# An adaLN block on one core: attention units, their background work, and where three of its jobs are put

## The chip, the cores and the metric

The kernel runs on one core of one Trainium2 chip. The metric is the device time of one execution in microseconds. The core has five engines with queues of their own: TensorE (PE, with PEld for its weight loads), VectorE (DVE), ScalarE (ACT), GpSimd (POOL), and SyncE (SP), which here issues nearly all DMAs.

## The reference

One transformer block with adaptive layer norms: S = 2048 tokens, D = 512, 32 heads of 16, F = 1792, all in fp32.

```python
mod = (_silu(c) @ w_mod).reshape(c.shape[0], 6, 1, -1)
sa, ca, ga, sb, cb, gb = (mod[:, 0], mod[:, 1], mod[:, 2], mod[:, 3], mod[:, 4], mod[:, 5])
h = _layernorm(x, axis=-1) * (1 + ca) + sa
x = x + ga * _A_ref(h, A_wqkv, A_wo)          # qkv, softmax(q k^T / 4) v, times wo
h = _layernorm(x, axis=-1) * (1 + cb) + sb
x = x + gb * _B_ref(h, B_w1, B_b1, B_w2, B_b2)  # gelu(h w1 + b1) w2 + b2
```

## The kernel before

Each large product is made of three products of the high and low parts of its factors (`terms3`): high·high, high·low, low·high.

**Units and half steps.** The attention is cut into 32 units: a block of 512 queries times a group of 4 heads (`NG` = 8 groups to a block, `NB` = 4 blocks). A unit has 16 half steps, so the main loop runs 512 (`half_step`). A half step issues on PE: 4 score matmuls `e`, transposed, keys by queries, with the exponential on ScalarE behind each; 4 score matmuls `mx` of a later unit (80 ahead, `LEAD`), with a reduction to the row's maximum on VectorE behind each; up to 6 background matmuls `bg`, on the two halves of the array's rows; and at its end the 4 matmuls `pv` of the half step before (`pv_step`), which the trace shows as 8 records. The maxima of a unit go through `max_rows` to DRAM (`m`) and from there into two rows of `qst`, so that the score matmul subtracts them itself. After the last `pv` of a unit `attn_out` copies the bank `pv` to `osb`, and a DMA takes it to `ou` in DRAM.

In the last 20 half steps there are no `mx` left; the code calls this "ending".

**Background.** A generator, `work`, hands out jobs: first the projections of q, k and v that are still missing (`block0`), then for each block of tokens the output projection with its layer norm (`front`) and the feed-forward (`feed`). A job is a group of matmuls into one bank; a group of 24 half-row matmuls takes four half steps. Where a generator yields nothing, because what it needs isn't there, the half step has no background. What is left when the loop is over runs in the tail on the full array, and there the last block follows: its output projection (`part_o`, bank `o`), layer norm and feed-forward. The numbers of `feed` groups in the tail are those that the loop didn't get to.

**Clock.** `advance` counts 4 per half step. `later(n, f)` runs f n counts on; `soon(n, f)` likewise, in its own order. All engines are fed in the order in which the program is written, so such a delay is a place in an engine's queue, and an instruction that must wait holds up what stands behind it there.

**Heads before the output projection.** When two groups of a block are out, a pair goes to `ready`, 8 counts after its `osb`; `o_prep(b, k)` then loads the sums `dn` and the values `ob` from `ou`, takes the reciprocal on VectorE (`inv`, 14 counts later, 20 for the first three of block 0), stores it to `rden` (`store`), loads it spread over rows (`load`, `rb`) and divides on GpSimd (`div`, 7 counts after the load). `done[b]` counts what is divided; `front` waits until all four are, and 4 counts more.

**Weights.** `wload` issues the next load of the list `stream` into one of 8 slots (`WB`), as soon as a slot has been dropped. Before the change the four tiles of wo for block b+1 stand ahead of the last part of block b's feed-forward weights. `open_ffn` opens the pool in which these slots lie, once the projections' own pools can be closed; the first four tiles of wo follow it.

**Layer norm of `front`.** Behind each of four groups the evacuation (`y`), the addition to x, the statistics in two halves on VectorE (`stat`, moved by `calm` where `max_rows` has just been), and the normalisation `xn`; then four transposes (`trans`), for block 0 as jobs of their own in empty half steps, for the others as `sides`, in a bank of the ring `mx` beside a half step's work.

Of the kernel before, what the change touches and what calls it, by code (L numbers as in the profile page):

```python
# [10 lines left out]
AF = mybir.ActivationFunctionType  # L11
# [11 lines left out]
NF = FF // P  # L23
# [36 lines left out]
Y202.a X1 x*2  # L60
"""
RUN = 6
WB = 8
FIRST = {"h32": 4, "pf": 1, "vr": 3}
STAGE = {"pf": 1, "vr": 1, "wraw": 2, "wf": 1}
# [6 lines left out]
def block_kernel(ctx: ExitStack, tc: tile.TileContext, x, wqkv, wo, w1, b1, w2, b2, c, w_mod, out):  # L72
# [233 lines left out]
        hi, lo = ([a[:, i].rearrange("p (k q c) -> p q k c", q=4, k=4) if blocks else a[:, i] for i in n] for a in hT[b])  # L306
        return terms3([t[:, 0, i] for i in n], [t[:, 1, i] for i in n], hi, lo)

    def proj_qk(w, k, b):
        def evac(ps):  # L310
            parts, r = pieces("parts"), stage("pf")
            ac.activation(r, ps, AF.Copy)
            gp.tensor_copy(parts[:, 0], r)
            gp.tensor_tensor(parts[:, 1], r, parts[:, 0].bitcast(F32), op=ALU.subtract)
            soon(6, lambda: store_qk(w, k, b, parts))

        return proj_terms(w, k, b), "bg", evac

# [378 lines left out]
        return act  # L697

    done = [-1] * NB
    ready = []  # L700

    def attn_out(u, pv):
        qb, g = divmod(u, NG)
        o = kqpool.tile([P, TB], F32, tag="osb", name="osb", bufs=1)
        saw(ac.activation(o, pv, AF.Copy))  # L705
        late = u < NU - 1
        later(2 * late, lambda: sy.dma_start(ou_d[qb][g], o))
        if g % 2:
            later(8 * late, lambda: ready.append((qb, g // 2)))

    def pv_step():
        s = cur["pv"]
# [38 lines left out]
    def o_prep(b, k):  # L751

        dn = small.tile([P, 32], F32, tag="dn", name="dn")
        base = ou_d[b]
        sy.dma_start(dn, base[2 * k : 2 * k + 2].rearrange("g (j r) (a f) -> (g j) r a f", r=32, f=32)[:, DH])
        ob, rb = tmp("ob"), tmp("rb")
        for g in range(2):
            sy.dma_start(ob[g * 64 : (g + 1) * 64], base[2 * k + g].rearrange("(j r) t -> j r t", r=32)[:, :DH])
        eng = ve if over[0] else gp
        r = rden_d[b][k * 8 : (k + 1) * 8]  # L760
        busy[0] += 1

        def inv():
            ve.reciprocal(dn, dn)
            later(0 if over[0] else 2, store)

        def store():
            sy.dma_start(r.rearrange("h (a f) -> (h a) f", f=32), dn)
            later(1 if over[0] else 5, load)
            if over[0]:  # L770
                wload()

        def load():
            sy.dma_start(rb, bass.AP(tensor=r.tensor, offset=r.offset, ap=[[TB, 8], [0, DH], [1, TB]]))
            later(9 if over[0] else 7, div)
            if over[0]:
                for _ in range(6):
                    wload()
                load_x2(last, x2)

        def div():
            eng.tensor_tensor(ob, ob, rb, op=ALU.mult)
            eng.tensor_copy(pc(b, k, 0), ob)
            eng.tensor_tensor(pc(b, k, 1), ob, pc(b, k, 0).bitcast(F32), op=ALU.subtract)
            done[b] += 1
            busy[0] -= 1

        later(11 if over[0] else 20 if b == 0 and k < KC - 1 else 14, inv)

    def try_prep():  # L790
        if not ready or not pcs:
# [15 lines left out]
    for b in range(NB):  # L807
        at = 0
        for lo, hi, top in PARTS:
            if hi == NF and b < NB - 2:  # L810
                stream += [(b + 1, "o", k) for k in range(KC)]
            stream += [(b, 1, i) for i in range(at, top)] + [(b, 2, i) for i in range(lo, hi)]
            at = top
        if b == NB - 2:
            stream += [(b + 1, "o", k) for k in range(KC)]
    wt, used, ringed, extra = {}, set(), [], []

# [34 lines left out]
    def front(b, x2):  # L852


        later(9, lambda: load_x2(b, x2))
        yield from until(lambda: done[b] == KC - 1)
        yield from wait(4)
        yield from loaded(b, *[("o", k) for k in range(KC)])
        mv = small.tile([P, 4, 2], F32, tag="mv", name="mv")
        rs = {}  # L860
        xn = {}

        def norm(t):
            xn[t] = tmp("xn")
            (gp if b or t < 3 else ve).tensor_scalar(
                xn[t], x2[t], mv[:, t, 0:1], rs[t], op0=ALU.subtract, op1=ALU.mult)
            later(40, lambda: gp.tensor_tensor(x2[t], x2[t], b2_b, op=ALU.add))
            if b and len(xn) == 4:
                later(9, lambda: sides.extend([lambda fc=fc: trans(fc, "mx") for fc in range(KC)]))

        def stat(t):
            if b == 0 and t == 3:
                ln_stat(mv, t, x2[t])
                later(1, lambda: factor(t))
                return
# [12 lines left out]
            calm(lambda: [part(0), later(4, lambda: calm(lambda: [part(1), later(4, whole)]))])  # L888

        def factor(t):  # L890
            rs[t] = small.tile([P, 1], F32, tag=f"rt{t}", name=f"rt{t}")
            ve.tensor_scalar(rs[t], mv[:, t, 1:2], EPS, None, op0=ALU.add)
            gp.tensor_tensor(rs[t], rs[t], mhalf[:, 0:1], op=ALU.pow)
            later(3 if t < 3 else 2, lambda: norm(t))

        for t in range(4):

            def evac(ps, t=t):
                y = tmp("y")
                ac.activation(y, ps, AF.Copy)  # L900

                def add():
                    gp.tensor_tensor(x2[t], y, x2[t], op=ALU.add)
                    later(8 if b or t < 3 else 3, lambda: stat(t))
# [5 lines left out]
        t0 = clock["t"]  # L910

        def trans(fc, bk="bg"):
            ps = take(bk)
            for t in range(4):
                te.transpose(ps[:, t * P : (t + 1) * P], xn[t][:, fc * P : (fc + 1) * P], ident)  # L915
            h = tmp("h32")
            ac.activation(h, ps, AF.Identity, scale=modc[:, 1, fc, 0:1], bias=modc[:, 1, fc, 1:2])
            gp.tensor_copy(pc(b, fc, 0), h)
            gp.tensor_tensor(pc(b, fc, 1), h, pc(b, fc, 0).bitcast(F32), op=ALU.subtract)
            turned[fc] = clock["t"]  # L920

        turned = {}
        yield "ln"
        if b:
            yield from until(lambda: len(turned) == KC and clock["t"] >= turned[KC - 1] + 8)
            return
        yield from until(lambda: len(xn) == 4 and clock["t"] >= t0 + 9)
        for fc in range(KC):
            yield lambda fc=fc: trans(fc)
        yield from wait(4)  # L930

    def feed(b, x2):

# [47 lines left out]
        for lo, hi, top in PARTS:  # L981
# [11 lines left out]
            for t in range(4):  # L993
                sl = slice(t * P, (t + 1) * P)

                def evac(ps, t=t):
                    add_x2(ps, t)
                    if hi == NF:
                        r0 = b * TB + t * P
                        later(2 if over[0] else 8, lambda: sy.dma_start(out[r0 : r0 + P, :], x2[t]))  # L1000

                yield [(gt[i][0][:, a, sl], wt[b, 2, i][:, c]) for i in range(lo, hi) for a, c in three], "bg", evac
            drop(b, *[(2, i) for i in range(lo, hi)])

    def block0():
# [13 lines left out]
        for n, (w, k, bs) in enumerate(plan):  # L1019
            if not pcs and not any(0 in p[2] for p in plan[n:]):  # L1020
                open_pc()
            yield from until(lambda: (w, k) in wt_of)
            fetch(n + 2)
            for b in bs:
                yield proj_v(k, b) if w == 2 else proj_qk(w, k, b)
            wt_of.pop((w, k))
        yield from until(lambda: not preps and not owed[0] and not blocked and not vrows and not busy[0])
        open_ffn()

    pools["old"] = [dvcm, scm, wcm, hcm]  # L1030

# [2 lines left out]
    def work():  # L1034
# [3 lines left out]
        for b in range(NB - 1):  # L1038
            for j in fronts[b]:
                if j != "ln":  # L1040
                    yield j
            for j in feed(b, pools["x2"][b % 2]):
                if j != "last":
                    togo[0] -= b == NB - 2 and j is not None
                    yield j
                elif b < NB - 2:
                    for i in fronts[b + 1]:
                        if i == "ln":
                            break
                        yield i  # L1050

    jobs = work()
    act = {"g": None}
# [290 lines left out]
```

## Time and profile before

| | |
|---|---|
| runs | 1674.72, 1675.60, 1676.36 us; median 1675.6 |
| profiled execution | 1677.1 us |
| its span | 1675.3 us |
| granted TensorE clock, mean | 0.997 |
| busy: PE, PEld | 1654.6 us (99%), 899.8 us (54%) |
| busy: DVE, ACT, POOL | 1406.9 us (84%), 1227.6 us (73%), 701.6 us (42%) |
| DMA | 246.95 MB, 147 GB/s on average |
| VectorE's reductions L419 | 2034 of 681 ns |
| ScalarE's exponentials L691 | 2048 of 609 ns |
| ScalarE's copies `osb` L705 | 32 of 601 ns |

Times in rows are microseconds from the start of the span. A row of the timeline gives start, duration, engine, line, operation, output and inputs, shape and count, and in brackets how long the engine stood before it and what released it. PE's matmuls are pipelined, so neighbouring rows overlap, and the start of one `pv` burst to the start of the next is the length of a half step.

### The profile page before, as it was taken

The numbers are of one execution on the slowest core, as the hardware profiler recorded it, in microseconds if no ns is written. First come the engines' busy times: TensorE is split into PE (matmuls) and PEld (weight loads), VectorE is DVE, ScalarE is ACT, GpSimd is POOL, SyncE is SP. The second block draws the span as 40 slices with busy tenths as digits, with TensorE's granted clock in tenths as the row PEclk, the third lists the DMA queues.
The fourth block names the chain that finished last, engine by engine and source line by source line (L and its number), as shares of the span: only waits on it lengthen the run. The fifth ranks groups of instructions, "written<-read, shape, count | busy, mean of one in ns | idle before, by whom it ended". The sixth has DMA issues, their size and how long they took to land.

```text
span 1675.3 us, 32208 instructions
## 1 busy us (share of the span) xinstructions
PE 1654.6 (99%) x12055; PEld 899.8 (54%) x12055; DVE 1406.9 (84%) x2734; ACT 1227.6 (73%) x2352; POOL 701.6 (42%) x705
## 2 busy tenths in 40 slices
PE   7999999999999999999999999999999999999999
PEld 6655555555554455555545555555545555553777
DVE  7899899998898998898999888998999888890432
ACT  4357777777777788778877888778877788779131
POOL 8343544535121556306533456306533366226110
PEclk9999999999999999999999999999999999999999
DMA  9766766766447444336363364345363453233544
GB/s 298 204 198 181 229 206 208 226 178 199 140 138 213 119 106 116 77 83 167 96 168 87 101 162 119 81 106 157 101 170 88 123 143 99 70 117 97 218 151 154
DMA packets 142808, 246.95 MB, mean 147 GB/s; under 512 B 25391, under 2 KB 53053, under 8 KB 142653
## 3 DMA queue, kind: packets, MB, share of 16 engines
q1 hardware_dynamic: 140896, 243.80, 50.4%
q8 instruction: 95, 1.56, 0.4%
q10 hardware_dynamic: 1756, 1.11, 0.3%
q14 instruction: 61, 0.49, 0.1%
HBM read 184.56 MB, written 60.29 MB: 146 GB/s over the span
## 4 chain that ended last, share of the span: by engine, by line
PE 94%; DVE 2%; DMA 2%; ACT 2%; issue 0%; SPq 0%; POOL 0%; POOLq 0%; DVEq 0%; ACTq 0%
PE bg L278 40%; PE pv L717 29%; PE e L684 17%; PE mx L414 4%; PE pr L278 2%; ACT p L691 1%; DVE mxp L419 1%; PE o L278 1%; PE warm L466 1%; DMA w2s<-wsp 1%; DMA dn<-ou 0%; DVE bst L236 0%; PE mx L915 0%; DMA qk<-parts 0%; DMA wo<-wos 0%
## 5 line engine op out<-in xcount | busy, mean ns | idle before, releaser
L419 DVE TENSOR_REDUCE mxp<-mx 128x1 f32<-128x512 f32 x2034 | 1284.8, 681 | 128.2 <-PE mx L414 108.5
L691 ACT ACTIVATE p<-e 128x512 f32<-128x512 f32 x2048 | 1073.1, 609 | 275.6 <-PE mx L414 233.1
L414 PE MATMUL mx<-kh,qst 48*128 48x512 f32 x2034 | 836.6, 423 | 0.7 <-DVE mxp L419 0.5
L684 PE MATMUL e<-qst,kh 50*128 50x512 f32 x2048 | 779.5, 424 | 3.3 <-ACT p L691 3.3
L684 PEld LDWEIGHTS e<-qst,kh 50*128 50x128 f32 x2048 | 341.8, 185 | 438.3 <-ACT p L691 325.6
L717 PE MATMUL pv<-p,vg 128*17 128x512 f32 x4096 | 540.0, 598 | 0.3 <-ACT osb L705 0.3
L414 PEld LDWEIGHTS mx<-kh,qst 48*128 48x128 f32 x2034 | 368.2, 185 | 16.2 <-DVE mxp L419 9.3
L278 PE MATMUL bg<-w,g 64*128 64x512 f32 (+1 forms) x1056 | 264.4, 389 | 0.0
L278 PEld LDWEIGHTS bg<-w,g 64*128 64x128 f32 (+1 forms) x1056 | 196.0, 186 | 29.0
L278 PE MATMUL bg<-pchi,w 64*128 64x512 f32 (+1 forms) x656 | 178.0, 391 | 0.0
L717 PEld LDWEIGHTS pv<-p,vg 128*17 128x17 f32 x4096 | 68.2, 95 | 174.3 <-issue 171.8
L278 PE MATMUL bg<-hThi,wqkv 64*128 64x512 f32 x560 | 153.4, 393 | 0.2 <-DVE tick L1149 0.2
L278 PEld LDWEIGHTS bg<-pchi,w 64*128 64x128 f32 (+1 forms) x656 | 120.9, 185 | 23.4 <-DVE tick L1127 4.3
L278 PEld LDWEIGHTS bg<-hThi,wqkv 64*128 64x128 f32 x560 | 103.7, 186 | 12.7 <-DVE tick L1149 0.5
L959 POOL TENSOR_SCALAR s<-s 128x512 f32<-128x512 f32 x40 | 59.9, 1497 | 101.8 <-ACT s L957 101.4
L978 POOL TENSOR_TENSOR x<-y,x 128x512 f32<-128x512 f32 x28 | 36.0, 1286 | 148.0 <-ACT y L977 148.0
L278 PE MATMUL bg<-pclo,w 64*128 64x512 f32 (+1 forms) x328 | 88.9, 389 | 0.0
L278 PE MATMUL bg<-hTlo,wqkv 64*128 64x512 f32 x280 | 76.2, 391 | 0.0
L952 POOL TENSOR_TENSOR s<-h 128x512 f32<-128x512 f32 x40 | 41.7, 1042 | 65.2 <-ACT h L951 65.2
L278 PEld LDWEIGHTS bg<-pclo,w 64*128 64x128 f32 (+1 forms) x328 | 60.0, 184 | 13.2 <-DVE tick L1127 4.3
L278 PE MATMUL bg<-wo,pchi 64*128 64x512 f32 x192 | 60.2, 394 | 1.6 <-DMA wo<-wos 1.6
L278 PEld LDWEIGHTS bg<-hTlo,wqkv 64*128 64x128 f32 x280 | 51.6, 184 | 7.7
(165 smaller groups left out, 1313.6 us busy)
## 6 DMA issues: line engine op xcount, KB each, us to landing
kh<-qk SPq DMA_DIRECT2D x256, 192.0 KB
w<-w1s SPq DMA_DIRECT2D x56, 512.0 KB
w<-w2s SPq DMA_DIRECT2D x54, 512.0 KB
qk<-parts SPq DMA_DIRECT2D x32, 512.0 KB
vg<-v SPq DMA_DIRECT2D x48, 272.0 KB
qst<-qk SPq DMA_DIRECT2D x64, 192.0 KB
qk<-parts SPq DMA_DIRECT2D x32, 256.0 KB
ou<-osb SPq DMA_DIRECT2D x32, 256.0 KB
```

The source lines that it names most:

```text
L278: return te.matmul(ps, term[0][r], rhs, start=i == 0, stop=i == n - 1)
L414: te.matmul(ps, qst[u][r0 : r0 + KR, p, qc * P : (qc + 1) * P], kh(u, kr // 2)[r0 : r0 + KR, p, (kr % 2) * TB : (kr % 2 + 1) * TB], start= ...
L419: ins = ve.tensor_reduce(mxp[u][:, hc, kr : kr + 1], ps, axis=AX.X, op=ALU.max, negate=True)
L466: te.matmul(warm[:, :P], ident, ident, start=True, stop=True)
L684: ins = te.matmul(ps, kh(u, kc // 8)[r0 : r0 + KX, p, (kc % 8) * P : (kc % 8 + 1) * P], qst[u][r0 : r0 + KX, p], start=True, stop=True)
L691: op = ac.activation(t, ps, AF.Exp, scale=SCALE)
L717: te.matmul(pvb[32 * j : 32 * j + VW], vg[u % 2][:, n : n + VW], pt.pop(4 * s + j), start=kc == 0, stop=kc == NKC - 1)
L952: gp.tensor_tensor(s, h, h, op=ALU.mult)
L959: gp.tensor_scalar(s, s, 1.0, None, op0=ALU.add)
L978: later(4, lambda: gp.tensor_tensor(x2[t], y, x2[t], op=ALU.add))
```

## The change

Six things change, and no computation is left out.

- `attn_out` copies the bank `pv` to `osb` on VectorE rather than ScalarE, and `calm` takes note of it.
- The chain of the heads: for the last pair of blocks 1 and 2, ready 4 counts rather than 8 after `osb`, reciprocal 9 rather than 14, division 3 rather than 7; for the first three pairs of block 0, reciprocal 28 rather than 20. `front` no longer waits for the division plus 4 counts, but for a mark set 2 counts after the load of `rb`.
- wo's tiles: for block 0 the four loads are issued right behind `open_ffn`, that is when the pools change, followed by a wait of 12 counts (`OPEN`); the last projection's store goes out at once, so that the pool can open. For the later blocks wo(b+1) stands behind all of block b's weights in the list, and is asked for at the yield "last".
- `work` lets the feed-forward of block b go on with a group wherever the front of block b+1 has nothing yet at its beginning.
- The transposes of block 0, too, go into `sides`, 5 rather than 9 counts after the last `xn`, and `front` goes on when three of four have been issued.
- Delays of statistics and of the addition of b2 are changed, and the slots of w2 of a block's last part are dropped one after another.

```diff
+OPEN = 12
-    def proj_qk(w, k, b):
+    def proj_qk(w, k, b, last=False):
-            soon(6, lambda: store_qk(w, k, b, parts))
+            soon(0 if last else 6, lambda: store_qk(w, k, b, parts))
...
+    close_by = [False] * NB
...
-        saw(ac.activation(o, pv, AF.Copy))
+        saw(ve.tensor_copy(o, pv))
+        rowed[0] = clock["t"]
         late = u < NU - 1
         later(2 * late, lambda: sy.dma_start(ou_d[qb][g], o))
         if g % 2:
-            later(8 * late, lambda: ready.append((qb, g // 2)))
+            later((4 if 0 < qb < NB - 1 and g == NG - 1 else 8) * late, lambda: ready.append((qb, g // 2)))
...
-            later(9 if over[0] else 7, div)
+            later(9 if over[0] else 3 if fast else 7, div)
+            if k == KC - 1:
+                later(2, lambda: close_by.__setitem__(b, True))
...
-        later(11 if over[0] else 20 if b == 0 and k < KC - 1 else 14, inv)
+        fast = 0 < b < NB - 1 and k == KC - 1
+        later(11 if over[0] else 28 if b == 0 and k < KC - 1 else 9 if fast else 14, inv)
...
-            if hi == NF and b < NB - 2:
-                stream += [(b + 1, "o", k) for k in range(KC)]
             stream += [(b, 1, i) for i in range(at, top)] + [(b, 2, i) for i in range(lo, hi)]
             at = top
-        if b == NB - 2:
+        if b < NB - 1:
             stream += [(b + 1, "o", k) for k in range(KC)]
...
-        yield from until(lambda: done[b] == KC - 1)
-        yield from wait(4)
+        yield from until(lambda: close_by[b])
...
-            later(40, lambda: gp.tensor_tensor(x2[t], x2[t], b2_b, op=ALU.add))
-            if b and len(xn) == 4:
-                later(9, lambda: sides.extend([lambda fc=fc: trans(fc, "mx") for fc in range(KC)]))
+            later(40 if b else 72, lambda: gp.tensor_tensor(x2[t], x2[t], b2_b, op=ALU.add))
+            if len(xn) == 4:
+                later(5, lambda: sides.extend([lambda fc=fc: trans(fc, "mx") for fc in range(KC)]))
...
-            calm(lambda: [part(0), later(4, lambda: calm(lambda: [part(1), later(4, whole)]))])
+            n = 4 if t < 3 else 3
+            calm(lambda: [part(0), later(n, lambda: calm(lambda: [part(1), later(n, lambda: calm(whole))]))])
...
-        if b:
-            yield from until(lambda: len(turned) == KC and clock["t"] >= turned[KC - 1] + 8)
-            return
-        yield from until(lambda: len(xn) == 4 and clock["t"] >= t0 + 9)
-        for fc in range(KC):
-            yield lambda fc=fc: trans(fc)
-        yield from wait(4)
+        yield from until(lambda: len(turned) >= KC - 1)
...
+                if t == 3 and hi == NF and b < NB - 2:
+                    for n, i in enumerate(range(lo, hi)):
+                        later(7 + 4 * n, lambda i=i: drop(b, (2, i)))
...
         open_ffn()
+        for k in range(KC):
+            wload()
+        yield from wait(OPEN)
...
-            for j in feed(b, pools["x2"][b % 2]):
+            fd = feed(b, pools["x2"][b % 2])
+            for j in fd:
...
                 elif b < NB - 2:
+                    first = True
+                    for k in range(KC):
+                        wload()
                     for i in fronts[b + 1]:
                         if i == "ln":
                             break
-                        yield i
+                        first = first and i is None
+                        yield next(fd) if first else i
```

How this moves instructions, at three places. On SP, ahead of unit 9, where block 0's wo is asked for. `qk<-parts` are the projection's last stores, `m` and `qst<-m` the maxima on their way, `kh` keys, `w` tiles of w1. Before:

```order
L301 DMA qk_86<-parts 128x512
L441 DMA m_104<-m_7429 4x32x32 x2
L300 DMA qk_86<-parts 128x2x512
L301 DMA qk_86<-parts 128x512
L447 DMA qst<-m_104 2x1024 x2
L386 DMA kh_194<-qk_88 48x2x512 x2
L831 DMA wo<-wos_135 128x1024
```

Now:

```order
L301 DMA qk_86<-parts 128x2x512
L302 DMA qk_86<-parts 128x512
L835 DMA wo<-wos_135 128x1024
L835 DMA wo<-wos_136 128x1024
L835 DMA wo<-wos_137 128x1024
L835 DMA wo<-wos_138 128x1024
L442 DMA m_104<-m_7431 4x32x32 x2
L835 DMA w_7498<-w1s_139 128x1024
L448 DMA qst<-m_104 2x1024 x2
L387 DMA kh_194<-qk_88 48x2x512 x2
```

The maxima's store and load have moved behind the four tiles of wo.

On PE, from the last `pv` of the loop into the tail; `pchi` and `pclo` are the parts of the feed-forward's input, `g` those of its inner layer. Before:

```order
L717 MATMUL pv<-p,vg_1176 17x512 x8
L278 MATMUL bg<-pchi_5322,w_22616 128x512 x8
L278 MATMUL bg<-pclo_5323,w_22616 128x512 x4
L278 MATMUL bg<-pchi_5322,w_22702 128x512 x8
L278 MATMUL bg<-pclo_5323,w_22702 128x512 x4
L278 MATMUL bg<-w_22792,g 128x512 x3
```

Now:

```order
L720 MATMUL pv<-p,vg_1176 17x512 x8
L279 MATMUL bg<-w_22523,g 128x512 x3
L279 MATMUL bg<-w_22615,g 128x512 x3
L279 MATMUL bg<-w_22704,g 128x512 x3
L279 MATMUL bg<-w_22790,g 128x512 x3
L279 MATMUL bg<-w_22523,g 128x512 x3
```

Two groups of the first layer, 24 matmuls, have left the tail.

On DVE, at a unit change in the second half of the loop, as it stands now; before, the same place has the reductions alone:

```order
L1157 COPY tick<-mx 128x1
L420 TENSOR_REDUCE mxp<-mx 128x1
L707 COPY osb<-pv 128x512
L420 TENSOR_REDUCE mxp<-mx 128x1 x7
L1157 COPY tick<-mx 128x1
```

The copy has come between the last reduction of a half step and the first of the next.

More of the change, by code (lines that the diff above doesn't have):

```diff
@@ L903, in add @@
                     gp.tensor_tensor(x2[t], y, x2[t], op=ALU.add)
-                    later(8 if b or t < 3 else 3, lambda: stat(t))
+                    later(8 if t < 3 else 4 if b else 3, lambda: stat(t))
                 later(2, add)
@@ L909, in front, with trans @@
         drop(b, *[("o", k) for k in range(KC)])
-        t0 = clock["t"]
-        def trans(fc, bk="bg"):
+        def trans(fc, bk):
             ps = take(bk)
@@ L1024, in block0 @@
             for b in bs:
-                yield proj_v(k, b) if w == 2 else proj_qk(w, k, b)
+                yield proj_v(k, b) if w == 2 else proj_qk(w, k, b, n == len(plan) - 1 and b == NB - 1)
             wt_of.pop((w, k))
```

## The prediction

> **What bounds the kernel now.** I read the page first: busy shares, then the chain that ended last. Then the timeline of PE, which I cut at the pv matmuls, because each half step ends with one burst of eight.
>
> ```profile
> PE 1654.6 (99%) x12055; PEld 899.8 (54%) x12055; DVE 1406.9 (84%) x2734; ACT 1227.6 (73%) x2352; POOL 701.6 (42%) x705
> PE bg L278 40%; PE pv L717 29%; PE e L684 17%; PE mx L414 4%; PE pr L278 2%; ACT p L691 1%; DVE mxp L419 1%; PE o L278 1%; PE warm L466 1%; DMA w2s<-wsp 1%; DMA dn<-ou 0%; DVE bst L236 0%; PE mx L915 0%; DMA qk<-parts 0%; DMA wo<-wos 0%
> ```
>
> PE is busy for 99% and the chain lies on it, so time is only won where PE stands, runs at a lower clock, or does background matmuls in the tail that a half step could have taken. The price list comes from distances between pv bursts:
>
> ```profile
> 1152.55 1.05 PE L717 MATMUL pv<-p,vg 128*17 128x512 f32 x8
> 1155.37 1.05 PE L717 MATMUL pv<-p,vg 128*17 128x512 f32 x8
> 1158.32 1.05 PE L717 MATMUL pv<-p,vg 128*17 128x512 f32 x8
> ...
> 862.89 1.05 PE L717 MATMUL pv<-p,vg 128*17 128x512 f32 x8
> 865.49 1.05 PE L717 MATMUL pv<-p,vg 128*17 128x512 f32 x8
> ```
>
> A half step with background takes 2.82 us (first pair; 2.83 is its usual value), one without it 2.60 (last pair; six such average 2.62). So background that fills an empty half step costs 0.21 there. The second pair, 2.95, is a unit change: 0.12 more.
>
> The profiled execution took 1677.1 us (span 1675.3), 1.5 above the median of 1675.6. I add differences to 1677.1 and take 1.5 off at the end. About 0.2%, 3.4 us, is what a measurement of this kernel can tell from no change.
>
> **Fill and tail.** By the order, 8 half steps of the loop that had no background now have it: 264 to 267, 396, 397, and two of 160 to 167. That is two groups of 24 half-row matmuls (12 full-row ones each), which leave the tail. There such matmuls run back to back:
>
> ```profile
> 1552.48 19.35 PE bg L278 x84
> 1571.83 10.91 PE o L278 x48
> ...
> 1565.65 0.69 DVE L782 TENSOR_TENSOR ob<-ob,rb 128x512 f32<-128x512 f32 x1 [4.02 <-DMA rb<-rden]
> ```
>
> 19.35/84 = 0.230 each, so 24 go for −5.5. The last head's division at 1565.65 and two more operations end near 1567.5; 18 of the 48 matmuls of the second row come ahead of its first user, which is at 1571.83 + 18 × 0.23 = 1576. Of these 8.5 us, 5.5 less leave 3. The projection's weights are asked for in the same tail; I give back 0.2 for them: **−5.3**, between −5.5 and −3. Six filled half steps outside 160 to 167 cost 6 × 0.21 = **+1.3**.
>
> ```profile
> 558.25 1.05 PE L717 MATMUL pv<-p,vg 128*17 128x512 f32 x8
> ...
> 570.86 1.05 PE L717 MATMUL pv<-p,vg 128*17 128x512 f32 x8
> 573.77 1.05 PE L717 MATMUL pv<-p,vg 128*17 128x512 f32 x8
> ...
> 582.17 1.05 PE L717 MATMUL pv<-p,vg 128*17 128x512 f32 x8
> ```
>
> Half steps 160 to 167 last 23.92 (first to last row). After, six are empty, four of these carry a transpose, and two are full. A step with a transpose takes 2.91 (second row to third). So 2 × 2.62 + 4 × 2.91 + 2 × 2.83 = 22.5. The first four take 12.61 now, where three empty ones and one with a transpose would take 10.77; if these 1.8 us of stalls return, the stretch takes 24.3. The same additions and statistics stand before the transposes, so I stay near the upper end: **+0.3**, between −1.4 and +0.4.
>
> **The divisions of the first heads.** Half step 107 is long because VectorE stands in front of a reciprocal whose DMA is not in:
>
> ```profile
> 404.14 1.05 PE L717 MATMUL pv<-p,vg 128*17 128x512 f32 x8
> 404.72 0.35 DVE L764 RECIPROCAL dn<-dn 128x32 f32<-128x32 f32 x1 [1.16 <-DMA dn<-ou]
> 407.95 1.05 PE L717 MATMUL pv<-p,vg 128*17 128x512 f32 x8
> ```
>
> 3.81 against 2.83. The delay 20 to 28 is two half steps, 5.6 us, against a wait of 1.16: gone, **−1.0**. The shorter delays (14 to 9) for the last head of blocks 1 and 2 could bring such a wait back twice: 0 to +2, taken as **+0.3**.
>
> **The copy of the pv bank, on VectorE.** Where it stood and what it cost:
>
> ```profile
> 1156.52 0.60 ACT L705 ACTIVATE osb<-pv 128x512 f32<-128x512 f32 x1 [0.39 <-PE pv L717]
> ...
> 1156.92 1.89 DVE L419 TENSOR_REDUCE mxp<-mx 128x1 f32<-128x512 f32 x3 [0.27 <-PE mx L414]
> ...
> L195 DVE COPY pf<-pr 128x512 f32<-128x512 f32 x1 | 0.7, 657 | 0.0
> ```
>
> ScalarE's copy pushes the next exponentials back and costs the 0.12 above. VectorE does such a copy in 0.66 (third row), some 0.58 from start to start with the overlap its neighbours show, and has an idle 0.27 just there (second row). So the next reduction is late by 0.3. What lateness costs is seen once:
>
> ```profile
> 179.68 1.05 PE L717 MATMUL pv<-p,vg 128*17 128x512 f32 x8
> ...
> 181.72 1.84 DVE L419 TENSOR_REDUCE mxp<-mx 128x1 f32<-128x512 f32 x3
> ...
> 182.85 1.05 PE L717 MATMUL pv<-p,vg 128*17 128x512 f32 x8
> ```
>
> In this half step the first reduction starts 2.04 after the pv burst (181.72 − 179.68), against 1.55 above (1156.92 − 1155.37): 0.49 late, behind the rows of the maxima. The half step takes 3.17, 0.34 too much. So lateness beyond some 0.15 passes to PE. At 0.3 that is 0.13 to 0.15: as much as ScalarE's copy costs now. Twenty of the 27 unit changes with reductions beside them thus come out at nothing. Seven meet other VectorE work there: three a pair of transposes, two a reciprocal, two half a statistic.
>
> ```profile
> 127.02 0.49 DVE L344 STREAM_TRANSPOSE vst<-vr 128x128 f32<-128x128 f32 x2
> ```
>
> A pair takes 0.42 from start to start and comes through whole, since the slack is used: 3 × 0.42. For the other four I take the reciprocal's 0.35 (row above), 0.28 from start to start: 4 × 0.28. Together **+2.4**. Below, the copy is free and 27 × 0.12 is won: −3.2. Above, the idle 0.27 isn't there, and each of the twenty costs 0.3: +8. I take the middle because the idle stands in the row.
>
> At the end there are no reductions, and the copy is plainly won:
>
> ```profile
> 1517.85 1.05 PE L717 MATMUL pv<-p,vg 128*17 128x512 f32 x8
> 1520.36 1.05 PE L717 MATMUL pv<-p,vg 128*17 128x512 f32 x8 [0.33 <-ACT osb L705]
> 1522.77 1.05 PE L717 MATMUL pv<-p,vg 128*17 128x512 f32 x8
> 1524.87 0.62 PE L717 MATMUL pv<-p,vg 128*17 128x512 f32 x4
> ```
>
> 2.51 and 2.41 against 2.10: **−0.6**.
>
> **The output weights before unit 9.** The largest term, and the least sure.
>
> ```profile
> 509.26 1.05 PE L717 MATMUL pv<-p,vg 128*17 128x512 f32 x8
> ...
> 512.29 0.70 PE L278 MATMUL bg<-wo,pchi 64*128 64x512 f32 x1 [1.55 <-DMA wo<-wos]
> ...
> 518.37 1.05 PE L717 MATMUL pv<-p,vg 128*17 128x512 f32 x8
> ...
> 510.00:512.00 2.00, 0.74 (x6) 0.19 (x2) 1.39 (x3) 0.84 (x2) 0.00 (x0) 1.00 1.02 377
> 512.00:514.00 2.00, 1.71 (x8) 1.57 (x10) 0.48 (x1) 0.65 (x2) 0.00 (x0) 0.59 1.01 406
> 514.00:515.20 1.20, 1.20 (x10) 0.52 (x11) 0.90 (x2) 0.94 (x2) 0.00 (x0) 0.50 1.05 338
> 515.20:518.00 2.80, 2.80 (x21) 1.42 (x22) 1.78 (x4) 1.62 (x4) 0.00 (x0) 0.90 1.05 243
> ```
>
> The windows' last columns are granted clock, DMA share and GB/s. Half steps 144 and 145 last 9.11, 3.45 more than 5.66: 1.75 of waiting, and 1.7 of lower clock (0.41 × 2.0 + 0.5 × 1.2 + 0.1 × 2.8). The Trainium skill, "TensorE: Matmul & The Clock Gate" (Part 1 and the table behind "Why this matters for your kernels"), has the clock halve after an idle window of some 3.4 us and warns of gaps over some 3 us. Here the clock fell after a gap of 1.55 us, so I let the trace decide: a short stall also costs the 1.7. By the page a stall under 3 us would be 1.7 cheaper, which would move only the rival with the short stall.
>
> Now SP's queue there:
>
> ```profile
> 501.78 1.20 SPq L441 DMA_DIRECT2D m<-m  x2
> ...
> 503.55 0.46 SPq L301 DMA_DIRECT2D qk<-parts  x1
> 504.46 1.02 SPq L447 DMA_DIRECT2D qst<-m  x2
> ...
> 507.47 1.76 SPq L831 DMA_DIRECT2D wo<-wos  x4
> ...
> SPq L831 <- DMA qk<-parts: 1.0, 1, 1.0
> ```
>
> The first weight load waits for the last stores of qk to land (last row): 3.9 us from the second store's issue to its own. The change asks earlier and stores at once, so the second store goes out near 502.1 and the weights near 506.0 to 507.8. But by the order, the stores and all four weight loads now stand ahead of the maxima (m), and the loads of qst from m behind that. So m leaves at 507.8 rather than 501.78; quiet, it takes 2.7 us to the qst load (501.78 to 504.46), which goes out at 510.5 and lands near 512. The first score matmul of unit 9 needs it, and stands at 510.25 today. Without any queueing the stall is therefore only passed from one load to another: ±0. With the four weight tiles in front of it, 2.1 MB at 406 GB/s = 5.2 us, m lands after 513 and qst near 516.3: +4.0, and up to +5 with a longer spell of low clock. If the wait vanished altogether: −3.45. The windows show the DMA engines full (share 1.0) for as long as the weights flow, so I stand near the queued end: **+3.2**.
>
> The later additions of b2 and the dropped w2 slots go beside other POOL and SP work and are taken at 0: w1 for the filling groups is asked for two half steps, 5.7 us, before use.
>
> **Sum:** −5.3 + 1.3 + 0.3 − 1.0 + 0.3 + 2.4 − 0.6 + 3.2 = +0.6. 1677.1 + 0.6 − 1.5 = **1676.2**.
>
> **Rivals.** (1) The weights' wait really goes: m isn't late, or its consumer can wait. For it: DMAs of 16 and 8 KB need little room among 512 KB ones. Against it: the order puts m's issue 6 us later whatever the queue does. −3.45 instead of +3.2: 1676.2 − 6.65 = 1669.6. (2) VectorE becomes the bound at unit changes: the copy and the reductions behind it lose the idle 0.27. For it: VectorE is busy for 84%. Against it: the row with the idle. It decides from 0.13 us for each of the twenty; with 0.2 it gives 20 × 0.2 = +4.0 on top, 1680.2, slower than before. (3) The filling doesn't happen for free: the w1 load or the last head comes late, and the groups fill no more than what their waits cost. The −5.3 + 1.3 fall away: +4.0 on top, 1680.2, too. The order speaks against it, the 5.7 us for a load in a busy queue for it.
>
> **Chances.** Forecast, with queueing from none (1673.0) to full (1678.0), 0.42; rival 1, 0.34; rival 2, 0.14; rival 3, 0.10. Faster is rival 1, same the forecast, slower the other two. The range goes from 1668.5, rival 1 with a little of the free copy, to 1681.0, rivals 2 and 3; below lie both gains together, above the copy's upper end.
>
> **What would show it.** Right: PE's first matmul of the tail is a second-layer group; the score matmul of unit 9 waits for a DMA of m near 512 to 516; half step 107 at 2.83; unit changes near 2.95. Wrong: no wait and full clock before unit 9 (rival 1), unit changes of 3.1 or more throughout (rival 2), waits for w1 near half steps 294 and 422 (rival 3).

## The result, and the profile after

The changed kernel takes 1685.67 us (median of 4 runs, 1683.93 to 1688.71) against 1675.98 for the kernel before: a ratio of 1.006, interval 1.0041 to 1.0079. It is slower by 9.7 us, where the forecast said 1676.2 with a range up to 1681.0. Its profiled execution took 1683.93 us (span 1682.1), the lowest of its four and 6.8 above the profiled one of before. I first account for these 6.8; a second profile of the changed kernel, among the experiments, shows where its longer executions lose more.

The half steps, cut again at the pv bursts of both traces, differ in few places (us, after less before; the line of the pv matmul is now L720):

| place | forecast | measured |
|---|---|---|
| tail, two groups fewer | −5.3 | −4.3 |
| six filled half steps | +1.3 | +1.35 |
| 160 to 167 | +0.3 | +1.0 |
| 107, reciprocal | −1.0 | −0.97 |
| 268 and the faster last heads | +0.3 | −0.2 |
| unit changes on VectorE | +2.4 | +2.3 |
| the copy in the ending | −0.6 | −0.5 |
| 144 and 145 | +3.2 | +3.7 |
| 492 to 494 | none | +5.0 |
| the rest, ahead of the loop too | none | −0.6 |
| sum | +0.6 | +6.8 |

All eight terms of the forecast are right to within about 1 us (the ending's rows give 0.41 + 0.31 = 0.72, of which 0.6 was forecast). One place isn't in the forecast at all. The timeline of the changed kernel there, first ScalarE, then GpSimd, then PE:

```profile
1512.04 2.06 ACT L692 ACTIVATE p<-e 128x512 f32<-128x512 f32 x4 [0.77 <-PE mx L415]
1517.88 0.63 ACT L954 ACTIVATE s<-s 128x512 f32<-128x512 f32 x1 [3.77 <-POOL s L951]
1518.41 4.98 ACT L692 ACTIVATE p<-e 128x512 f32<-128x512 f32 x10
```

```profile
1503.16 1.30 POOL L787 TENSOR_TENSOR ob<-ob,rb 128x512 f32<-128x512 f32 x1 [2.77 <-PE pv L720]
...
1506.59 1.49 POOL L956 TENSOR_SCALAR s<-s 128x512 f32<-128x512 f32 x1
...
1510.22 1.29 POOL L959 TENSOR_TENSOR g<-h,g 128x512 fp32r<-128x512 f32 x1
1511.45 1.30 POOL L787 TENSOR_TENSOR ob<-ob,rb 128x512 f32<-128x512 f32 x1
1512.81 0.61 POOL L788 CAST kh<-ob 128x512 fp32r<-128x512 f32 x1
1513.51 1.29 POOL L789 TENSOR_TENSOR kh<-ob,kh 128x512 fp32r<-128x512 f32 x1
1514.75 1.04 POOL L949 TENSOR_TENSOR s<-h 128x512 f32<-128x512 f32 x1
1515.88 0.62 POOL L950 TENSOR_SCALAR s<-s 128x512 f32<-128x512 f32 x1
1516.58 1.26 POOL L951 TENSOR_TENSOR s<-s,h 128x512 f32<-128x512 f32 x1
```

```profile
1513.35 1.05 PE L720 MATMUL pv<-p,vg 128*17 128x512 f32 x8
1519.05 0.50 PE L685 MATMUL e<-qst,kh 50*128 50x512 f32 x1 [3.05 <-ACT p L692]
1519.47 1.05 PE L720 MATMUL pv<-p,vg 128*17 128x512 f32 x8
1522.32 1.89 PE L720 MATMUL pv<-p,vg 128*17 128x512 f32 x8
1525.26 1.05 PE L720 MATMUL pv<-p,vg 128*17 128x512 f32 x8
```

Read upwards. PE stands 3.05 us for an exponential. The exponentials stand behind the tanh of a feed-forward group (L954) on ScalarE, which waits 3.77 us for GpSimd. This group is number 10 of block 2. GpSimd has its input since 1508.5, but does its first three operations (L949 to L951) only from 1514.75 on. Two divisions of heads (L787 to L789) stand ahead of them, and between the two the second part of the group before (L956 to L959). The first division had itself waited 2.77 us. Before the change a group had its input at the same place in the loop, but the same divisions ended ahead of it, and no group's second part stood between them:

```profile
1500.03 1.30 POOL L784 TENSOR_TENSOR kh<-ob,kh 128x512 fp32r<-128x512 f32 x1
1502.01 1.04 POOL L952 TENSOR_TENSOR s<-h 128x512 f32<-128x512 f32 x1 [0.68 <-ACT h L951]
```

The first division is also a whole half step later than before, and the reason stands on SP. The first two rows are from the kernel before, the last three from the changed one:

```profile
1483.81 0.34 SPq L768 DMA_DIRECT2D rden<-dn  x1
1489.50 0.59 SPq L774 DMA_DIRECT2D rb<-rden  x1
...
1490.41 0.32 SPq L771 DMA_DIRECT2D rden<-dn  x1
1490.79 0.42 SPq L835 DMA_DIRECT2D w<-w2s  x1
1499.43 0.60 SPq L777 DMA_DIRECT2D rb<-rden  x1
```

The store of the reciprocals goes out in half step 483 both times. The load that needs it follows after 5.7 us before, after 9.0 us now. Now SP issues four weight loads between 1474 and 1491, where the kernel before issues none from 1468 to 1494, and the DMA engines are busy for 0.59 to 0.72 of the time between 1482 and 1494, against 0.24 to 0.31 between 1476 and 1487 before. That these loads hold up the small store is likely, but no run shows it alone.

Then the clock, in windows of the changed kernel (the third last column is the granted clock):

```profile
1518.00:1520.00 2.00, 0.95 (x9) 0.32 (x9) 0.16 (x1) 2.00 (x5) 1.66 (x2) 1.00 0.07 11
1520.00:1522.00 2.00, 2.00 (x16) 1.03 (x8) 0.00 (x0) 2.00 (x5) 1.85 (x3) 0.66 0.10 22
1522.00:1524.00 2.00, 2.00 (x10) 0.15 (x8) 0.16 (x1) 1.39 (x3) 1.41 (x2) 0.50 0.69 248
```

0.34 × 2 + 0.5 × 2 = 1.7 us are lost to it, as in half steps 144 and 145 of the kernel before. There, the changed kernel shows the forecast's queue:

```profile
506.37 1.75 SPq L835 DMA_DIRECT2D wo<-wos  x4
508.17 1.16 SPq L442 DMA_DIRECT2D m<-m  x2
...
514.32 0.57 SPq L448 DMA_DIRECT2D qst<-m  x2
```

```profile
510.11 1.05 PE L720 MATMUL pv<-p,vg 128*17 128x512 f32 x8
515.99 0.76 PE L685 MATMUL e<-qst,kh 50*128 50x512 f32 x1 [4.83 <-DMA qst<-m]
519.42 1.58 PE L720 MATMUL pv<-p,vg 128*17 128x512 f32 x8
...
522.87 1.05 PE L720 MATMUL pv<-p,vg 128*17 128x512 f32 x8
```

The 16 KB of m took 6.1 us to release the load of qst (508.17 to 514.32; 2.7 before), and unit 9's first score matmul stood until 515.99. The Trainium skill, "DMA: Bandwidth & Descriptors" (section "Queues, rings and completion order"), says that each DMA engine takes a ring's descriptors in order; the row agrees, small behind large.

The low clock lasts longer here than in the kernel before:

```profile
516.00:518.00 2.00, 2.00 (x9) 1.64 (x11) 0.87 (x2) 1.14 (x2) 0.00 (x0) 0.50 0.98 242
518.00:520.00 2.00, 2.00 (x12) 0.86 (x12) 1.68 (x4) 1.25 (x3) 0.00 (x0) 0.50 0.98 288
520.00:523.00 3.00, 3.00 (x26) 1.60 (x22) 2.18 (x5) 1.53 (x4) 0.00 (x0) 0.91 1.02 239
```

From 516 on, 0.5 × 2 + 0.5 × 2 + 0.09 × 3 = 2.3 us are lost to it, against 1.7 before. So the 3.7 of the table are 3.1 more of standing (4.83 against 1.75) and 0.6 more of low clock.

The unit changes, in the same trace: one with a pair of transposes ahead of the copy, and one without.

```profile
149.92 0.50 DVE L345 STREAM_TRANSPOSE vst<-vr 128x128 f32<-128x128 f32 x2
150.34 0.65 DVE L707 COPY osb<-pv 128x512 f32<-128x512 f32 x1
150.92 1.87 DVE L420 TENSOR_REDUCE mxp<-mx 128x1 f32<-128x512 f32 x3
...
1162.28 0.68 DVE L707 COPY osb<-pv 128x512 f32<-128x512 f32 x1
1162.88 2.48 DVE L420 TENSOR_REDUCE mxp<-mx 128x1 f32<-128x512 f32 x4
```

The first takes 3.34 us (2.95 before), the second 2.94, as before.

### The profile page after: what moved, and what is told of

Its sections match the earlier page's. It is cut to its first block, busy times and chain, and to the rows that moved or that the text cites. A ratio compares the mean times of both kernels' runs of the same rounds, so it can differ in the third digit from the quotient of the medians.

```text
span 1682.1 us, 32274 instructions
## 1 busy us (share of the span) xinstructions
PE 1656.0 (98%) x12079; PEld 905.8 (54%) x12079; DVE 1424.9 (85%) x2770; ACT 1211.3 (72%) x2320; POOL 716.7 (43%) x719
## 4 chain that ended last, share of the span: by engine, by line
PE 93%; DMA 3%; DVE 2%; POOL 1%; ACT 0%; SPq 0%; issue 0%; POOLq 0%; ACTq 0%; DVEq 0%
PE bg L279 40%; PE pv L720 29%; PE e L685 16%; PE mx L415 4%; PE pr L279 2%; DMA wraw<-in_A_wqkv_dram 1%; DVE mxp L420 1%; PE o L279 1%; DMA qk<-parts 0%; DVE hTlo L510 0%; PE mx L918 0%; DMA m<-m 0%; DMA wt<-wos 0%; POOL wqkv L210 0%; DMA qst<-m 0%
## 5 line engine op out<-in xcount | busy, mean ns | idle before, releaser
L720 PE MATMUL pv<-p,vg 128*17 128x512 f32 x4096 | 541.1, 599 | 0.1
L279 PE MATMUL bg<-w,g 64*128 64x512 f32 (+1 forms) x1080 | 269.7, 389 | 0.0
L279 PEld LDWEIGHTS bg<-w,g 64*128 64x128 f32 (+1 forms) x1080 | 200.4, 186 | 30.8 <-POOL g L958 0.9
L279 PE MATMUL bg<-pchi,w 64*128 64x512 f32 x672 | 182.9, 391 | 0.0
L720 PEld LDWEIGHTS pv<-p,vg 128*17 128x17 f32 x4096 | 68.2, 95 | 170.6 <-issue 168.8
L279 PEld LDWEIGHTS bg<-pchi,w 64*128 64x128 f32 x672 | 123.9, 185 | 23.0 <-DVE tick L1135 5.1
L956 POOL TENSOR_SCALAR s<-s 128x512 f32<-128x512 f32 x42 | 62.9, 1497 | 82.5 <-ACT s L954 81.7
L279 PE MATMUL bg<-pclo,w 64*128 64x512 f32 x336 | 91.9, 392 | 0.0
L949 POOL TENSOR_TENSOR s<-h 128x512 f32<-128x512 f32 x42 | 43.8, 1042 | 74.9 <-ACT h L948 74.9
L279 PEld LDWEIGHTS bg<-pclo,w 64*128 64x128 f32 x336 | 61.7, 185 | 14.5 <-DVE tick L1135 3.4
L437 POOL CAST m<-mt 128x32 fp32r<-128x32 f32 x32 | 6.8, 212 | 123.1 <-DVE mt L435 123.1
```

The source lines that it names most:

```text
L279: return te.matmul(ps, term[0][r], rhs, start=i == 0, stop=i == n - 1)
L437: gp.tensor_copy(m2[:, 0], mt)
L720: te.matmul(pvb[32 * j : 32 * j + VW], vg[u % 2][:, n : n + VW], pt.pop(4 * s + j), start=kc == 0, stop=kc == NKC - 1)
L949: gp.tensor_tensor(s, h, h, op=ALU.mult)
L956: gp.tensor_scalar(s, s, 1.0, None, op0=ALU.add)
```

## The experiments

Each set ran beside the kernel before on its own chip, whose median was 1678.39 in the first set, 1677.47 in the second, 1678.01 in the third and 1678.57 in the last; times compare within a set. "The changed kernel" is the base of every edit.

**A tanh later, the wrong one.**

```diff
-                later(9, second)
+                later(17 if (b, i) == (NB - 2, 12) else 9, second)
```

> The changed kernel, with one tanh of the feed-forward (first layer, group 12 of block 2) placed 17 instead of 9 counts behind its group, so two half steps later on ScalarE. Theory A: at half step 492 that tanh waits on ScalarE for GpSimd, which stands behind two head divisions of the last block (3.2 us each); exponentials queue behind the tanh, PE stands 3.05 us and then runs at half clock. Half steps 492 to 494 (11.91 us in the changed kernel, 6.87 before) fall to 6.9 to 7.3, the time by 4.5 to 5. Rival B: the stall comes from the last maxima or the switch to the ending at the same place, not from the tanh: 492 to 494 stay at 11 to 12 and the time stays within 1 us of the changed kernel.

1687.06 us, ratio 1.0051 (1.0036 to 1.0066). Half steps 492 to 494 take 13.98: no gain. The trace still shows a tanh that waits, 5.12 us, and it is that of group 10, not 12. So this run decides nothing between A and B; it was misplaced. It did show that the stall is longer when the head's DMAs are later: the load of rb left at 1501.03 here rather than 1499.43, and GpSimd's first division waited 4.13 us, against 2.77.

**No filling by feed-forward groups.**

```diff
-                        yield next(fd) if first else i
+                        yield i
```

> The changed kernel without the filling by feed-forward groups while the next front waits. Theory A (the two groups that moved into the loop brought group 12 beside the head divisions): half steps 492 to 494 return to about 6.9 (-5.0), the empty half steps at 264 to 267 and 396 to 397 return (-1.3), and the tail gets its groups back (+5.0 to +5.5): together within 2 us of the changed kernel, lower rather than higher. Rival B (the stall is not the groups' doing): 492 to 494 stay at 12, the time rises by 4.

1693.36 us, ratio 1.0095 (1.0076 to 1.0114): neither. 492 to 494 fell to 8.25, but the stall only moved: half step 490 rose from 2.84 to 4.96, where another tanh waits 2.38 us for GpSimd, and 495 from 2.11 to 3.45. Half steps 264 to 267 rose from 11.33 to 14.72 and 392 and 393 from 5.67 to 11.45; the tail stayed at 120.5. So the filling wasn't what shortened the tail: without it 262 and 263 are empty, and the output projection starts at 264 rather than 266. The groups did not move back, and theory A isn't decided by this run. The filling covers something else:

```profile
1228.40 2.19 SPq L835 DMA_DIRECT2D wo<-wos  x4
...
1233.01 0.68 PE L279 MATMUL bg<-wo,pchi 64*128 64x512 f32 x1 [2.06 <-DMA wo<-wos]
```

The rows are of half step 392. The change asks for wo(b+1) only at "last". Without a group between, its first user comes at once.

**The weights behind the maxima at the pool change.**

```diff
         open_ffn()
-        for k in range(KC):
-            wload()
+        gate[0] = True
+        def ask():
+            gate[0] = False
+            for k in range(KC):
+                wload()
+        later(9, ask)
         yield from wait(OPEN)
...
+        if gate[0]:
+            return
         if n == len(stream) or "f" not in pools:
```

> The changed kernel with the four loads of the output weights at the pool change issued 9 counts later, behind the store of the maxima m and the load of qst. Theory C: m queues behind 2.1 MB of weights and this alone holds unit 9; half steps 144 and 145 (12.76 us, 9.11 before) fall to 5.7 to 7, the time by 5.5 to 7. Rival D: the weights themselves cannot be in on time however the queue is ordered; 144 and 145 return to about 9.1, the time falls by 3.7.

1683.59 us, ratio 1.0034 (1.0021 to 1.0046). 144 and 145 take 12.15 instead of 12.76: a smaller gain than either theory said, and not much outside the 12.55 to 13.75 of the eight profiles that leave this place as it is. The maxima are in on time now, but

```profile
507.18 1.79 SPq L839 DMA_DIRECT2D wo<-wos  x4
...
513.78 0.76 PE L279 MATMUL bg<-wo,pchi 64*128 64x512 f32 x1 [3.47 <-DMA wo<-wos]
```

the weights are late by 3.47 us, more than by the 1.55 of before, and the low clock behind the stand costs 3.1 us, more than the 2.3 of the changed kernel. Of the two theories D comes nearer: in the three orders run so far the two are not both in by 510, and whichever goes second is waited for.

**The copy back on ScalarE.**

```diff
-        saw(ve.tensor_copy(o, pv))
-        rowed[0] = clock["t"]
+        saw(ac.activation(o, pv, AF.Copy))
```

> The changed kernel with the copy of the pv bank back on ScalarE. Theory E: VectorE's copy costs only where it meets other VectorE work (units 1, 3, 5 and half steps 112, 257, 385: 2.2 us in all), wins 0.5 us in the ending and is even elsewhere: the time falls by 1 to 2.5. Rival F: VectorE is the bound at all unit changes, so each of 27 gives back some 0.2 to 0.3: the time falls by 5 to 8.

1686.22 us, ratio 1.0043 (1.0028 to 1.0058). The time can't tell, as 492 to 494 take 13.27 in this run; the half steps can. Units 1, 3 and 5 fall from 10.02 to 8.82 together, 257 and 385 by 0.2 each, and the ending rises by 0.49. Half step 112 falls by 0.46, but it is short, 2.83, in the second profile of the changed kernel too, so that isn't the copy's doing. The mean of 21 unit changes without other work is 2.94, against 2.95 in the changed kernel. Theory E by the half steps, and not F: even, except where copies meet transposes or statistics.

**The right tanh later.** Group 10 at 21 counts.

```diff
-                later(9, second)
+                later(21 if (b, i) == (NB - 2, 10) else 9, second)
```

> The changed kernel with the tanh of group 10 of block 2 (the one that the trace shows waiting for GpSimd at half step 492; the run with group 12 moved another tanh) placed 21 instead of 9 counts behind its group, three half steps of the ending later. Theory A (GpSimd behind two head divisions, ScalarE in order behind the tanh): half steps 492 to 494 fall from 11.9 (14.0 in the run with group 12) to 6.9 to 7.5. Rival B (the last maxima, or the switch to the ending): they stay at 11 to 14.

1682.16 us, ratio 1.0027 (1.0014 to 1.004), against 1686.41 for the changed kernel in the same set. 492 to 494 fall to 6.89: A. But a new stall stands at 498 and 499 (7.77), where the next tanh waits 1.64 us for GpSimd, which now does group 10's second part ahead of group 11's first.

**Weights behind the maxima, and two half steps more.** The edit with `gate`, and

```diff
-OPEN = 12
+OPEN = 20
```

> The changed kernel with the weights behind m and qst as before, and the wait behind the pool change 20 instead of 12 counts, so that the output projection starts two half steps later. In the run with 12 counts PE then waited 3.47 us for the weights themselves. Theory C2 (m and the weights cannot both be in by half step 144; weights asked for at 507 land from 513 on): with two more half steps both are hidden, half steps 144 to 147 take 10.9 to 11.5 (two empty, two full) and no low clock is left; the changed kernel needs 18.4 there. Rival D2: the weights are later than that, and PE waits 1 us or more at half step 146. By theory A the shift of the groups by two half steps also moves group 10 clear of the divisions: half steps 492 to 494 at 6.9 to 7.5; by rival B they stay at 11 to 14.

1689.15 us, ratio 1.0073 (1.0057 to 1.0089). At its place it does what C2 says: 144 to 147 take 10.97 (18.24 in the changed kernel of the set). But the heads of block 1 are now ready when "last" comes, so nothing fills, and the weights are late:

```profile
852.81 2.11 SPq L839 DMA_DIRECT2D wo<-wos  x4
...
857.90 0.76 PE L279 MATMUL bg<-wo,pchi 64*128 64x512 f32 x1 [3.58 <-DMA wo<-wos]
```

Half step 264 takes 7.92, 392 takes 6.27. 492 to 494 fell to 8.24 rather than 7.5, and 490 rose to 5.53 and 495 to 3.50: in this order it is group 9 whose tanh waits. PE stands 2.23 us for it, and here the granted clock stays at 1.00.

**The changed kernel again.**

> The changed kernel again, on the chip of this set, to compare with the others and to see what differs between its runs (1683.9 to 1688.7 us). Theory: the spread comes from the stalls at half steps 144 and 492, which last as long as a DMA takes and end in a spell of low clock of varying length; elsewhere the half steps agree within 0.1 us. Rival: the spread is spread over the whole loop.

1686.41 us, ratio 1.0055 (1.0042 to 1.0068). Its profile is of a run of 1687.73, 3.8 above the first profile. 492 to 494 make 2.75 of that (14.66 against 11.91), and 2.1 lie ahead of the loop, where a load of qst is waited for (1.8 us); 144 and 145 are shorter by 0.2, and 112 by 0.6. At 492 both parts differ: PE stands 4.38 us instead of 3.05, and the half clock lasts 6.83 us instead of 3.41. So the theory is right for 492, wrong for 144, and missed the part ahead of the loop.

**Three edits at once:** `gate`, `OPEN` 20, the tanh of group 10 at 21, and ScalarE's copy for the first six units.

```diff
-        saw(ve.tensor_copy(o, pv))
-        rowed[0] = clock["t"]
+        if u < 6:
+            saw(ac.activation(o, pv, AF.Copy))
+        else:
+            saw(ve.tensor_copy(o, pv))
+            rowed[0] = clock["t"]
```

> Weights behind m with the wait of 20, the tanh of group 10 later, and the copy of the pv bank on ScalarE for the first six units, where it met transposes on VectorE. By theories A, C2 and E: the changed kernel less 7 at the pool change, less 5 at half step 492, less 1.2 at units 1, 3 and 5: some 13 us faster than the changed kernel, 3 to 6 us faster than the kernel before. Rival: the stalls come back elsewhere, and it is within 2 us of the kernel before or slower.

1687.88 us, ratio 1.0068 (1.0055 to 1.008): the rival. Each edit gains at its place (10.96 in 144 to 147, 8.80 in units 1, 3 and 5), and the stalls at 264 (7.13), 392 (7.23) and 490 (5.14) take it back.

**A group always ahead of the output projection,** on top of `gate` and `OPEN` 20.

```diff
+                        if first and i is not None and i != "ln":
+                            yield next(fd)
                         first = first and i is None
```

> The run with weights behind m and the wait of 20, and in addition one feed-forward group always goes between asking for the output weights and their first use, also where the heads are ready (in that run they were, no group filled, and PE waited 5 us for weights asked for at the same half step). Theory G (the filling is what covers the late request): the waits for the output weights at half steps 264 and 392 go (7.9 and 6.3 us fall to 2.8 to 2.9, with the low clock behind them, together 10 us), those of the tanhs at 490 and 494, by theory A from the divisions, stay. 1687.9 falls to 1677 to 1680. Rival H: the DMA queue at the unit change makes the weights late whenever they are asked for: 264 or 392, or the half steps four later, stay 1 us or more too long.

1676.64 us, ratio 0.9997 (0.9988 to 1.0006), against 1689.15 for the same kernel without that group in the set before. 264 and 392 take 2.83: G. 490 and 491 still take 10.43, as G said.

**Group 10 at 17 counts,** nothing else.

> The changed kernel with the tanh of group 10 at 17 instead of 9 counts, so that GpSimd does the first part of group 11 before the second part of group 10 (at 21 it did them the other way round, and group 11's tanh stood for 1.6 us at half step 498). Theory A: half steps 492 to 494 at 6.9 to 7.5 and 498 and 499 at 4.2 to 4.8 (7.8 at 21): 6 to 7.5 us faster than the changed kernel in the same half steps. Rival B: a stall of 3 us or more stays somewhere between 492 and 500.

1679.92 us, ratio 1.0013 (1.0004 to 1.0023). 492 to 494 take 7.08, half step 495 is 0.9 too long, and 498 and 499 are back at 4.2. From 492 to 501 that is 6.8 less than in the second profile of the changed kernel, and 4.1 less than in the first, whose stall is shorter.

**All mended.** `gate`, `OPEN` 20, the group ahead, ScalarE's copy for six units, and the tanh of group 9 at 17.

> All together: weights behind m, the wait of 20, the group that always goes ahead of the output projection, the copy of the pv bank on ScalarE for the first six units, and the tanh that by theory A stands behind the divisions in this order (group 9 of block 2, at half step 490) at 17 instead of 9 counts. By theories A, C2, E and G no stall over 1 us is left but those at 162 and 163: 4 to 7 us faster than the kernel before, so a ratio near 0.997. Rival: the stalls move on, and it is within 0.1% of the kernel before or slower.

1670.53 us, ratio 0.9964 (0.9952 to 0.9977): 7.5 below the kernel before, a little more than the 4 to 7 expected, and faster than both the kernel before and the changed one. Ahead of unit 9, on SP and PE:

```profile
501.79 1.57 SPq L442 DMA_DIRECT2D m<-m  x2
505.27 0.57 SPq L448 DMA_DIRECT2D qst<-m  x2
...
506.83 1.79 SPq L842 DMA_DIRECT2D wo<-wos  x4
...
513.69 1.05 PE L723 MATMUL pv<-p,vg 128*17 128x512 f32 x8
515.02 0.46 PE L279 MATMUL bg<-wo,pchi 64*128 64x512 f32 x1
...
516.64 1.05 PE L723 MATMUL pv<-p,vg 128*17 128x512 f32 x8
```

PE does not stand: the same loads, in this order and with 5 us more, are in.

**Only the divisions moved.**

```diff
-            later(9 if over[0] else 3 if fast else 7, div)
+            later(9 if over[0] else 3 if fast else 22 if b == NB - 1 and k < 2 else 7, div)
```

> The changed kernel with only the first two head divisions of the last block moved, 22 instead of 7 counts behind their load, so that GpSimd does the first part of group 10 ahead of both; its tanh stays where it is. Theory A in its full form (it is the divisions, with GpSimd standing for their DMA, that make group 10 late): half steps 492 to 494 fall from 12 to 14.7 to 6.9 to 7.5, and 1678 to 1682 in all. Rival I (nine counts are too few in the ending for GpSimd's three operations, divisions or not): the stall stays at 1.5 us or more.

1680.54 us, ratio 1.0014 (1.0002 to 1.0025). 492 to 494 take 6.87, as before the change. On GpSimd and ScalarE:

```profile
1507.00 1.04 POOL L949 TENSOR_TENSOR s<-h 128x512 f32<-128x512 f32 x1 [0.34 <-ACT h L948]
1508.13 0.62 POOL L950 TENSOR_SCALAR s<-s 128x512 f32<-128x512 f32 x1
1508.84 1.29 POOL L951 TENSOR_TENSOR s<-s,h 128x512 f32<-128x512 f32 x1
1510.07 1.30 POOL L787 TENSOR_TENSOR ob<-ob,rb 128x512 f32<-128x512 f32 x1
...
1512.36 0.65 ACT L954 ACTIVATE s<-s 128x512 f32<-128x512 f32 x1
```

The tanh stands where it stood, and waits for nothing. It is the place of the divisions, and rival I falls. How much of it is their own 6.4 us, how much the later load of rb and how much the second part that stood between them, this run doesn't separate.

## Why the prediction was wrong

**The step that failed** is "Fill and tail". It priced two groups that go from the tail into the loop by PE alone, 0.21 for each filled half step, and asked only what is late next in the tail. But a group is more than its 24 matmuls: its evacuation is seven operations on GpSimd and two on ScalarE, and moving the whole row of groups forward moves these against everything that has a time of its own, such as the divisions of the last block's heads. With 9 counts between a group's first part and its tanh, 6.4 us of divisions, which came late themselves and had another group's second part between them, were enough to hold ScalarE, and with it all exponentials: +5.0 us in one profile, +7.8 in the other. Moving the divisions alone removes it (6.87 in 492 to 494, 6.88 before the change); moving the tanh alone to 17 counts leaves 1.1 of it (7.08, and 0.9 in 495).

The sentence on the rest ("go beside other POOL and SP work and are taken at 0") failed in the same way: it looked at what was edited, not at what the shift brings together. The forecast's test for rival 3 looked for waits for w1; the wait was for GpSimd.

**The pool change** was right in mechanism and near in size: m behind four weight tiles, 3.7 against 3.2. The low clock came again, but not at one price: 2.3 us were lost to it after 4.83 us of standing here, 1.7 after 3.05 us at half step 492, 1.7 after 1.55 in the kernel before. The Trainium skill's rule ("TensorE: Matmul & The Clock Gate", the table behind "Why this matters for your kernels") of gaps over some 3 us fits the first two; the third had shown that shorter ones can do it too. The forecast's "a short stall also costs the 1.7" isn't a rule either: the stand of 2.23 us in the run with `OPEN` 20 cost none. That the loads can be hidden at all was left open in the forecast; only more time between them and their user does it, not the order alone.

**The unit changes** were right in kind: +0.40 at each of three transposes where 0.42 was said, and even elsewhere. The sum of 2.3 is partly luck: 0.62 of it is half step 112, which the second profile of the changed kernel doesn't show; without it the sum is 1.6. So the reciprocals' cost is not confirmed. Where half statistics were feared 257 and 385 show 0.2 each. **The ending** and **half step 107** were right. **The tail** gained 4.3 instead of 5.3, since part of the projection's weights is waited for there (1.0 us, where 0.2 had been given).

**Rival 1** did not happen; the traces show the queue that the order had shown. **Rival 2** fell with the run that puts the copy back. **Rival 3** had the right sign for the wrong cause.

The forecast put most of its doubt on the pool change and let the range end at 1681.0; a stall of 5 to 8 us from a chance meeting of two engines' work had no part in it, though the kernel before had one of 3.45 us at the pool change.

## What to carry to other kernels

When a change shifts hand-scheduled work, price it by every engine that the shifted jobs use: lay each engine's queue before and after side by side and look where an operation with a wait comes to stand ahead of one that the busiest engine needs. A request that is covered only because something else happens to be late loses its cover when that is mended, so the cover has to be put in on purpose. Improvements at one place should be judged by the half steps there and by the whole: three of them together gained nothing here until the late loads that they had uncovered were covered again and the tanh that waits in the new order was moved.

## What the runs showed of the hardware

A DMA of 16 KB issued behind 2.1 MB on the same queue took 6.1 us until its landing released the next instruction, against 2.7 to 3.5 without (501.78 to 504.46 in the kernel before, 502.14 to 505.62 in the run with the weights behind the maxima).

The half clock comes in spells of one length or a multiple of it. In the traces' clock records they last 3.41 us (half step 144 of the kernel before, half step 492 of the changed one), 6.83 (half step 144 of the changed kernel, 513.72 to 520.54) or 10.24 (the same place with the tanh of group 12 later). What a spell costs depends on how much of it falls behind the stand: 1.7 us of 3.41, 2.3 of 6.83 where PE stood until 515.99, 3.2 of 10.24. How long PE stands doesn't decide by itself whether one comes: 1.55 us drew one in the kernel before, 2.23 us at half step 490 with `OPEN` 20 drew none.
